# Attention with expert routing: the turned rows of blocks 3 and 4 placed in another step, and a routing written with other instructions

## The chip, the cores and the metric

The kernel runs on one core of one Trainium2 chip. Five engines work side by side and meet through semaphores: TensorE (PE, whose weight loads are listed as PEld), VectorE (DVE), ScalarE (ACT), GpSimd (POOL) and SyncE (SP, which issues most DMAs). The metric is the device time of one execution in microseconds (us).

## What is computed

Attention with rotary positions for 4 batches, 8 heads, 576 tokens and 64 numbers a head, and behind it a sparse feed-forward layer with 8 experts. The reference, cut:

```python
# attention, for every batch and head
q_rot, k_rot = rotate(q), rotate(k)
attn = softmax(q_rot @ k_rot.T / sqrt(64))
x = (attn @ v)            # heads side by side: (4, 576, 512)

# one expert a token
logits = x @ w_gate                      # (4, 576, 8)
local_gate = sigmoid(x @ w_local)        # (4, 576)
for b, s:
    fresh_e = argmax(logits[b, s])
    e = fresh_e if s == 0 or local_gate[b, s] < 0.5 else prev_e
    prev_e = e
    p = softmax(logits[b, s])[e]
    out[b, s] = p * (relu(x[b, s] @ w1[e]) @ w2[e])
```

A token whose local gate is 0.5 or more keeps the expert of the token before it, so the experts of a batch follow from a scan over its 576 tokens.

## The kernel before

**Attention.** Two heads are a pair; there are 16 pairs (4 a batch), and each takes 9 steps, so step g = 0 to 143 is step i = g mod 9 of pair p = g div 9. (Counted from one, i = 5 is the sixth step.) A step makes the scores of one tile of 128 queries by 576 keys (`mm_s`, tile `s`, two PSUM buffers of pool `ps_s`), takes each row's minimum on DVE (`softmax_min`, `mn`; the scores carry a minus sign), the exponential and its row sum on ACT (`softmax_exp`, `e` or `et`, `sum`), turns the exponentials of two steps earlier on PE (`tr_main`, `tm`, `tk`, `tt`), splits them into a high part on ACT (`pth`, `pkh`) and a low part on DVE (`ptl`, `pkl`), and multiplies with the values of the pair before (`pv_mm`, five products a step by `PV_STEPS`, none in i = 8; `pv_evac` adds the halves: `tmp` on ACT, `xt` on DVE). The tiles tm, tk, tt, pv and gx share the four PSUM buffers of pool `ps_t`. POOL rotates and splits the queries, keys and values of coming pairs (`stage`, `xq`, `xk`, `v`).

**Turned rows.** Two pairs later, `gates(p)` divides by the row sums and turns the finished rows back to token order, which also gives the gate logits: `sums` (ACT and a RECIPROCAL on DVE), `rows(0, 3)` for blocks 0 to 2 of 128 tokens and `rows(3, 2)` for blocks 3 and 4. `rows` makes products on PE into a PSUM tile `gx`; for pairs 0 to 10 the first call copies gx on ACT and multiplies on POOL, the second multiplies on DVE from PSUM (`gm`, 36 numbers a partition, then `xrow`, 256). The rows go to DRAM (`rows_d`). The main loop appends these functions to a list `soon` at step `GATES_AT` and takes one from it in each step: before, sums in i = 7, rows(0, 3) in i = 8, rows(3, 2) in i = 0 of the next pair.

**Routing.** When 12 of 16 pairs are turned, `route(0, 3)` routes batches 0 to 2 (15 blocks of 128 tokens) in the steps that the string `ORDER` gives, from g = 121 (pair 13) on and in the drain behind the last step: `fresh` (best expert and the key of each token that doesn't keep its neighbour's), `last_reset` (the scan), `experts` (expert numbers, one-hot, counts), `ranks` (place of each token in its expert's list), `sums`, `probs`, then from `early` the plan of 6 tiles of 128 tokens with one expert each and from `slots` the token numbers of each slot (`gidx` to gather, `sidx` to scatter). `route(3, 1)` does the last batch's 5 blocks during the first experts.

**Experts.** 19 tiles: gather the rows (POOL), turn (`tx`, split to `xs`), first product (`h`), relu, turn (`th`, split to `hs`), second product (`o`), scale, scatter. Weights are loaded by SP and split into two parts by ACT, DVE and POOL (`split_w`).

**Order.** PE's instructions are meant to stand as written; DVE, ACT, POOL and SP are placed by a scheduler between step 12 and the end of attention, and it takes PE's instructions of neighbouring steps out of the written order in some places. PE and DVE stand as written during experts 0 to 5, all engines behind that. Each engine works through its own queue in order, so an instruction that waits holds what is queued behind it.

Of the kernel before, what the change touches and what calls it, by code (L numbers as in the profile page):

```python
# [17 lines left out]
ALU = mybir.AluOpType  # L18
# [6 lines left out]
P = 128  # L25
# [28 lines left out]

ORDER = ".....fs.rRe.klx.c0pt...wg.1.G"
BIG = 4096.0
# [6 lines left out]
ZTHR = -1.5 * 2.0 ** -23  # L63

_COLS = {}
_off = 0
for _n, _w in (
    ("iota128", 128), ("code8", 8), ("p1", 1),
    ("keys", NBLK * NE), ("s0", NBLK), ("pad", NBLK), ("tok64", NBLK),
    ("scan0", 8 * NG + 8), ("tile128", 25),  # L70
):
    _COLS[_n] = (_off, _off + _w)
    _off += _w
# [3 lines left out]
def _constants():  # L77
    c = np.zeros((P, NCONST), np.float32)
    p = np.arange(P)

    def put(name, a):
        lo, hi = _COLS[name]
        if a.dtype == np.int32:
            c.view(np.int32)[:, lo:hi] = a
        else:
            c[:, lo:hi] = a

    put("iota128", np.arange(128)[None])
    put("code8", 7 - np.arange(8)[None])
    put("p1", p[:, None] + 1)  # L90
    tok = np.zeros((P, NBLK))
    tok64 = np.zeros((P, NBLK))
    s0 = np.zeros((P, NBLK))
    pad = np.zeros((P, NBLK))
    s0[0, ::NB] = 1
    pad[:64, 4::NB] = 64
    for b in range(B):
        for j in range(NB):
            lo = b * S + (j * 128 if j < 4 else S - 128)
            tok[:, b * NB + j] = lo + p  # L100
            tok64[:, b * NB + j] = lo // 64
    put("keys", (TWO23 + 8 * tok[:, :, None] + 7 - np.arange(8)).reshape(P, -1))
    put("s0", s0)
    put("pad", pad.astype(np.int32))
    put("tok64", tok64)
# [32 lines left out]
def tile_attention_moe(ctx, tc, qk, v, tabs, turn, consts, tri, wg, wts, out):  # L138
# [17 lines left out]
    cst = const.tile([P, NCONST], F32, name="cst")  # L156
    C = {n: cst[:, a:b] for n, (a, b) in _COLS.items()}
    trib = const.tile([P, P], BF16, name="trib")
# [258 lines left out]
    def gates(p):  # L417
# [48 lines left out]

        def last_rows():
            rows(3, 2)
            for f in stores:
                f()  # L470

        return [sums, lambda: rows(0, 3), last_rows]

    def scores(b):

        g = gm_t[b]
        if b < B - 1:
            pool.tensor_tensor(g[:, :, 0:4], g[:, :, 0:4], g[:, :, 4:8], op=ALU.add)
            pool.tensor_tensor(g[:, :, 0:2], g[:, :, 0:2], g[:, :, 2:4], op=ALU.add)
            pool.tensor_tensor(lg_all[:, b * NB:(b + 1) * NB], g[:, :, 0], g[:, :, 1], op=ALU.add)  # L480
        else:
            dve.tensor_reduce(lg_all[:, 0:NB], g.rearrange("p j h e -> p j e h"), axis=AX.X, op=ALU.add)

    def route(b0, nb):
# [9 lines left out]
        def fresh():  # L494
# [16 lines left out]
            dve.scalar_tensor_tensor(c8, d, 0.0, keys, op0=ALU.is_equal, op1=ALU.mult)  # L511
            rs = blk("rs")
            dve.scalar_tensor_tensor(rs, lg[:, :, 8], ZTHR, C["s0"][:, cs], op0=ALU.is_lt, op1=ALU.max)
            yield
# [3 lines left out]
            key = blk("key")  # L518
            dve.tensor_tensor(key, rs, f, op=ALU.mult)
            yield  # L520
# [23 lines left out]
        def experts():  # L544
# [11 lines left out]

            dve.tensor_scalar(tcode[:, cs], e, -7.0, 4096.0, op0=ALU.add, op1=ALU.mult)
            cnt = small([P, NE, NG + 1], "cnt", BF16)
            dve.tensor_tensor(cnt[:, :, 1:n + 1].rearrange("p e j -> p j e"), bc(C["code8"], 1, n), bc(e, 2, 8), op=ALU.is_equal)
            dve.tensor_tensor(oh, bc(C["code8"], 1, n), bc(e, 2, 8), op=ALU.is_equal)  # L560

# [12 lines left out]
            cox_t[b0] = cox  # L574
            st["cnt"] = cnt

        def sums():
            se = blk("se")
            dve.tensor_reduce(se, st["ex"], axis=AX.X, op=ALU.add)
            yield  # L580
            dve.tensor_scalar(se, se, 1e-9, None, op0=ALU.add)
            yield
            dve.reciprocal(se, se)
            yield
            st["se"] = se

        def probs():
# [3 lines left out]
            p = blk("p")  # L591
            dve.tensor_reduce(p, pm, axis=AX.X, op=ALU.add)
            yield
            dve.tensor_tensor(p, p, st["se"], op=ALU.mult)
# [8 lines left out]
        def ranks():  # L603
# [14 lines left out]
            yield  # L618
            dve.tensor_tensor(o, r, hi, op=ALU.subtract)
            if final:  # L620
# [4 lines left out]
            yield  # L625
            dve.scalar_tensor_tensor(tcode[:, cs], hi, -TWO23, tcode[:, cs], op0=ALU.add, op1=ALU.add)
            yield
# [21 lines left out]
    def slots(codes, nblk, first, n):  # L649
# [3 lines left out]
        def spread_tokens():  # L653
# [9 lines left out]

            dve.tensor_tensor(rhs[:, 0], w, bc(C["tok64"][:, 0:nblk], 2, n), op=ALU.mult)
            dve.tensor_scalar(rhs[:, 1], w, C["p1"], None, op0=ALU.mult)
            yield
            st["rhs"] = rhs

        def gather_tokens():
# [6 lines left out]
            dve.tensor_scalar(hi, ps[:, 0], 64.0, None, op0=ALU.mult)  # L676
            yield
            dve.tensor_tensor(hi, hi, ps[:, 1], op=ALU.add)
            yield
            dve.tensor_copy(gidx[:, first:first + n], hi)  # L680
            pad = small([P, n], "ipad")
# [4 lines left out]

        return [spread_tokens, gather_tokens]

# [25 lines left out]
    take = const.tile([P, NE + 1], F32, name="take")  # L714
    after = const.tile([P, NE], F32, name="after")
    ex_row = const.tile([1, KE + NLATE + 1], F32, name="ex_row")


    def early():
# [4 lines left out]
        def plan():  # L724
# [469 lines left out]
    if True:  # L1194
# [40 lines left out]
        for g in range(NSTEP):  # L1235
            if g == GM:
                begin.close()
            with tc.manual_schedule(engines=None if g < GM else MAN0):
# [152 lines left out]
```

## Time and profile before

| what | value |
| --- | --- |
| median of 3 runs | 541.94 us (541.6 to 542.74) |
| the profiled execution | 541.58 us, span 539.7 us |
| busy PE, DVE, ACT, POOL | 517.0, 381.9, 347.2, 341.3 us (96, 71, 64, 63% of the span) |
| granted TensorE clock | 0.994 of full speed over the span |
| attention, routing 0 to 2, drain | about 0 to 297 us |
| experts, with the routing of batch 3 in the first ones | about 297 to 537 us |

The 541.58 us are the time of the profiled execution, of which the profile's records span 539.7. A busy share of PE near 100% hides little pauses, since the ends of matmuls are modelled; the distance between equal places of two pairs is the surer measure, and a bracket at a row's end gives the idle time ahead of an instruction and what ended it.

### The profile page before, as it was taken

The numbers are of one execution on the slowest core, as the hardware profiler recorded it, in microseconds if no ns is written. First come the engines' busy times: TensorE is split into PE (matmuls) and PEld (weight loads), VectorE is DVE, ScalarE is ACT, GpSimd is POOL, SyncE is SP. The second block draws the span as 40 slices with busy tenths as digits, with TensorE's granted clock in tenths as the row PEclk, the third lists the DMA queues.
The fourth block names the chain that finished last, engine by engine and source line by source line (L and its number), as shares of the span: only waits on it lengthen the run. The fifth ranks groups of instructions, "written<-read, shape, count | busy, mean of one in ns | idle before, by whom it ended". The sixth has DMA issues, their size and how long they took to land.

```text
span 539.7 us, 10708 instructions
## 1 busy us (share of the span) xinstructions
PE 517.0 (96%) x3273; PEld 458.5 (85%) x3273; DVE 381.9 (71%) x703; ACT 347.2 (64%) x762; POOL 341.3 (63%) x267
## 2 busy tenths in 40 slices
PE   7989999999999999998899999999999999999993
PEld 4889999999999999997888788887888888888882
DVE  6998999999999999999999935428422637421631
ACT  4988999999999999987676523353533443532440
POOL 4998989989969989896598302337511455411332
PEclk9999999999999999999999999999999999999997
DMA  8659698887886969977278205471637496637350
GB/s 275 279 132 230 183 246 231 209 192 216 217 229 134 233 189 235 223 189 171 39 200 230 83 20 177 125 267 49 225 103 238 125 353 151 203 100 234 84 172 26
DMA packets 63611, 97.37 MB, mean 180 GB/s; under 512 B 28146, under 2 KB 38898, under 8 KB 61747
## 3 DMA queue, kind: packets, MB, share of 16 engines
q1 hardware_dynamic: 60066, 86.48, 58.1%
q0 software_dynamic: 3040, 9.71, 5.6%
q8 instruction: 28, 0.46, 0.4%
q14 instruction: 45, 0.36, 0.2%
q10 hardware_dynamic: 432, 0.36, 0.2%
HBM read 76.98 MB, written 12.86 MB: 166 GB/s over the span
## 4 chain that ended last, share of the span: by engine, by line
PE 72%; DVE 10%; POOL 5%; DMA 4%; issue 4%; ACT 3%; SPq 1%; POOLq 0%; DVEq 0%; ACTq 0%
PE h L952 18%; PE o L995 17%; PE pv L361 12%; PE s L267 10%; PE tm L325 8%; DVE mn L272 3%; PE gx L435 2%; DVE ptl L307 2%; PE th L986 2%; DMA rows_d<-xrow 2%; PE tx L938 1%; POOL stage L196 1%; PE tk L335 1%; ACT e L289 1%; DMA qst<-xq 1%
## 5 line engine op out<-in xcount | busy, mean ns | idle before, releaser
L995 PE MATMUL o<-w,hs 128*128 128x512 f32 x456 | 112.9, 397 | 0.0
L272 DVE TENSOR_REDUCE mn<-s 128x1 f32<-128x576 f32 x144 | 107.2, 744 | 2.4 <-PE s L267 0.9
L952 PE MATMUL h<-w,xs 128*128 128x512 f32 x444 | 106.1, 392 | 0.8 <-DVE xs L307 0.5
L289 ACT ACTIVATE e<-s,mn 128x576 f32<-128x576 f32 x128 | 95.4, 746 | 14.8 <-DVE mn L272 12.0
L307 DVE TENSOR_TENSOR ptl<-tm,pth 128x512 fp32r<-128x512 f32 x139 | 95.3, 686 | 12.4 <-ACT pth L303 7.4
L1001 POOL DMA_INDIRECT out_dram<-os,sidx x19 | 23.1, 1214 | 123.6 <-ACTq L903 70.3
L267 PE MATMUL s<-m,qst 128*128 128x288 f32 x512 | 95.7, 309 | 4.5 <-ACT e L289 3.0
L952 PEld LDWEIGHTS h<-w,xs 128*128 128x128 f32 x444 | 82.5, 188 | 19.1 <-DVE w L897 1.1
L995 PEld LDWEIGHTS o<-w,hs 128*128 128x128 f32 x456 | 83.0, 188 | 16.9 <-DVE hs L307 0.4
L303 ACT CAST pth<-tm 128x512 fp32r<-128x512 f32 x139 | 80.9, 582 | 12.8 <-PE tm L325 11.8
L267 PEld LDWEIGHTS s<-m,qst 128*128 128x128 f32 x512 | 74.5, 188 | 8.4 <-ACT e L289 5.3
L361 PE MATMUL pv<-pth,v 128*128 128x288 f32 x256 | 76.8, 315 | 2.4 <-DVE pkl L307 1.3
L325 PE MATMUL tm<-wid,e 128*128 128x128 f32 x512 | 77.0, 272 | 0.6 <-ACT e L289 0.5
L361 PE MATMUL pv<-ptl,v 128*128 128x288 f32 x256 | 76.5, 314 | 0.0
L196 POOL TENSOR_TENSOR stage<-stage 128x1152 f32<-128x1152 f32 x26 | 69.1, 2667 | 4.4 <-DMA stage<-in_qk_dram 4.4
L325 PEld LDWEIGHTS tm<-wid,e 128*128 128x128 f32 x512 | 62.1, 140 | 1.2 <-ACT e L289 0.7
L897 DVE TENSOR_TENSOR w<-stage,w 128x1024 fp32r<-128x1024 f32 x37 | 51.0, 1412 | 15.6 <-ACT w L894 9.8
L361 PEld LDWEIGHTS pv<-pth,v 128*128 128x128 f32 x256 | 48.2, 188 | 6.0 <-issue 3.0
L361 PEld LDWEIGHTS pv<-ptl,v 128*128 128x128 f32 x256 | 48.3, 189 | 0.0
L307 DVE TENSOR_TENSOR xs<-tx,xs 128x512 fp32r<-128x512 f32 x19 | 13.1, 688 | 44.6 <-ACTq L903 35.0
L307 DVE TENSOR_TENSOR hs<-th,hs 128x512 fp32r<-128x512 f32 x26 | 17.5, 687 | 30.6 <-ACTq L903 18.9
L197 POOL TENSOR_TENSOR stage<-stage 128x576 f32<-128x576 f32 x26 | 37.0, 1430 | 0.3
(201 smaller groups left out, 821.4 us busy)
## 6 DMA issues: line engine op xcount, KB each, us to landing
stage<-in_wts_dram SPq DMA_DIRECT2D x84, 512.0 KB
stage<-in_qk_dram SPq DMA_DIRECT2D x13, 1152.0 KB
qst<-xq SPq DMA_DIRECT2D x56, 128.0 KB
stage<-in_v_dram SPq DMA_DIRECT2D x16, 320.0 KB
m<-xq SPq DMA_DIRECT2D x14, 288.0 KB
m<-xk SPq DMA_DIRECT2D x14, 288.0 KB
m<-xq SPq DMA_DIRECT2D x14, 256.0 KB
m<-xk SPq DMA_DIRECT2D x14, 256.0 KB
```

The source lines that it names most:

```text
L196: engine.tensor_tensor(x, x, tab[:, 2 * f:2 * f + 2], op=ALU.mult)
L197: engine.tensor_tensor(rr[:, f], x[:, 0], x[:, 1], op=ALU.add)
L267: pe.matmul(st[:, h, lo:hi], lhs, keys[:, k0:k0 + hi - lo], start=(n == 0), stop=(n == len(parts_) - 1))
L272: dve.tensor_reduce(mn, s_t[g][:, :, 0:HALF], axis=AX.XY, op=ALU.min)
L289: act.activation(dst.rearrange("p (h s) -> p h s", h=2), s_t.pop(g)[:, :, 0:HALF], AF.Exp, bias=mn, scale=-1.0, accum_out=sums[:, col:col ...
L303: act.copy(hi, src)
L307: dve.tensor_tensor(lo, src, hi.bitcast(F32), op=ALU.subtract)
L325: pe.transpose(ps[:, k], src[:, k * P:(k + 1) * P], ident)
L361: pe.matmul(pv_t[p, u], lhs.rearrange("p c d -> p (c d)"), rhs, start=(n == 0), stop=(n == 9))
L897: (pool if k in on_pool else dve).tensor_tensor(lo, src, hi.bitcast(F32), op=ALU.subtract)
L952: pe.matmul(ps[:, c], xs_t[t][:, x, k], w[y][:, c * 512:(c + 1) * 512], start=(k == 0 and n == 0), stop=(k == 3 and n == 2))
L995: pe.matmul(ps, hs_t[t][:, x, k], w[y][:, (k % 2) * 512:(k % 2 + 1) * 512], start=(k == 0 and n == 0), stop=(k == 7 and n == 2))
```

## The change

Five things are changed.

1. **The step of the turned rows.** For pairs below `POOL_ROWS` the list is now sums, rows(3, 2), nothing, nothing, rows(0, 3), store; and it is appended at i = 4 instead of 7 (pairs 13, 14 and 15 of the main loop keep their steps). So rows(3, 2) of pair p stands in i = 5 of pair p + 2, rows(0, 3) in i = 8 as before, and the store of its rows in i = 0.
2. **Left out or joined on DVE.** `rs` (a mask with the first token of a batch forced) is gone: the first token's local logit is overwritten by a one-element memset behind `lg_all`, on POOL for batches 0 to 2, and `key` compares and multiplies at once. The early `tcode` is gone: one operation at the end of `ranks` makes the code, with constants moved into `SHIFT` and `lead`. The two products that make `rhs` (tile `ex`, later `slr`) are one, over a constant of two halves.
3. **Moved to ACT.** The one-hot `oha` is a copy of `cnt`, and the 1e-9 is added to `se` there.
4. **Moved to POOL.** `lc` (for batches 0 to 2) and a new one-element `lead`.
5. **Order and types.** `gidx` comes from an addition that writes integers directly, not from a cast of `ihi`; the two operations of `sidx` are a function of their own (`i`, last in ORDER); `iota128` is bf16.

```diff
-ORDER = ".....fs.rRe.klx.c0pt...wg.1.G"
+ORDER = ".....fs.rRe.klx.c0pt...wg.1.Gi"
...
+SHIFT = TWO23 + 7 * 4096.0
...
-        return [sums, lambda: rows(0, 3), last_rows]
+        if p < POOL_ROWS:
+            rest = lambda: None
+            return [sums, lambda: rows(3, 2), rest, rest, lambda: rows(0, 3), lambda: stores[0]()]
+        return [sums, lambda: rows(0, 3), lambda: rows(3, 2)]
...
+            pool.memset(lg_all[0:1, b * NB:b * NB + 1, 8:9], -1.0)
...
-            rs = blk("rs")
-            dve.scalar_tensor_tensor(rs, lg[:, :, 8], ZTHR, C["s0"][:, cs], op0=ALU.is_lt, op1=ALU.max)
...
-            dve.tensor_tensor(key, rs, f, op=ALU.mult)
+            dve.scalar_tensor_tensor(key, lg[:, :, 8], ZTHR, f, op0=ALU.is_lt, op1=ALU.mult)
...
-            dve.tensor_scalar(tcode[:, cs], e, -7.0, 4096.0, op0=ALU.add, op1=ALU.mult)
             cnt = small([P, NE, NG + 1], "cnt", BF16)
             dve.tensor_tensor(cnt[:, :, 1:n + 1].rearrange("p e j -> p j e"), bc(C["code8"], 1, n), bc(e, 2, 8), op=ALU.is_equal)
-            dve.tensor_tensor(oh, bc(C["code8"], 1, n), bc(e, 2, 8), op=ALU.is_equal)
+            act.copy(oh, cnt[:, :, 1:n + 1].rearrange("p e j -> p j e"))
...
-            dve.tensor_scalar(se, se, 1e-9, None, op0=ALU.add)
-            yield
-            dve.reciprocal(se, se)
+            act.add(se, se, 1e-9)
...
             dve.tensor_reduce(p, pm, axis=AX.X, op=ALU.add)
+            dve.reciprocal(st["se"], st["se"])
...
-            dve.tensor_tensor(o, r, hi, op=ALU.subtract)
+            (dve if final else pool).tensor_tensor(o, r, hi, op=ALU.subtract)
...
-            dve.scalar_tensor_tensor(tcode[:, cs], hi, -TWO23, tcode[:, cs], op0=ALU.add, op1=ALU.add)
+            dve.scalar_tensor_tensor(tcode[:, cs], st["e"], 4096.0, hi, op0=ALU.mult, op1=ALU.add)
...
-            dve.tensor_tensor(rhs[:, 0], w, bc(C["tok64"][:, 0:nblk], 2, n), op=ALU.mult)
-            dve.tensor_scalar(rhs[:, 1], w, C["p1"], None, op0=ALU.mult)
+            tokp = C["tokp"].rearrange("p (c j) -> p c j", c=2)[:, :, 0:nblk]
+            dve.tensor_tensor(rhs, bc(w, 1, 2), bc(tokp, 3, n), op=ALU.mult)
...
+            dve.tensor_tensor(gidx[:, first:first + n], hi, ps[:, 1], op=ALU.add)
             dve.tensor_tensor(hi, hi, ps[:, 1], op=ALU.add)
             yield
-            dve.tensor_copy(gidx[:, first:first + n], hi)
+            st["hi"] = hi
+
+        def scatter_tokens():
+            hi = st["hi"]
             pad = small([P, n], "ipad")
...
+            pool.tensor_scalar(lead, take[:, 0:1], SHIFT, None, op0=ALU.add)
...
-                if i == GATES_AT.get(p, 7) and p >= 2:
+                if i == GATES_AT.get(p, 4) and p >= 2:
```

How the instructions stand is shown at three places. The first is PE in steps 2 and 3 of pair 8 (tiles s_75 and s_76), before; pairs 9 to 13 read alike:

```order
L267 MATMUL s_75_2531<-m_8_2179,qst0_99 128x288 x4
L325 MATMUL tm_72_2541<-wid_93,et_8_2453 128x128 x4
L341 MATMUL tt_72_2548<-wid_93,et_8_2453 128x128
L267 MATMUL s_76_2565<-m_8_2179,qst0_99 128x288 x4
L361 MATMUL pv_7_0_2554<-pth_7_2246,v2_7_2009 128x288
L361 MATMUL pv_7_0_2554<-ptl_7_2247,v2_7_2009 128x288
```

The same place now:

```order
L266 MATMUL s_75_2533<-m_8_2189,qst0_99 128x288 x4
L324 MATMUL tm_72_2543<-wid_93,et_8_2463 128x128 x4
L340 MATMUL tt_72_2550<-wid_93,et_8_2463 128x128
L360 MATMUL pv_7_0_2556<-pth_7_2248,v2_7_2011 128x288
L360 MATMUL pv_7_0_2556<-ptl_7_2249,v2_7_2011 128x288
```

The scores s_76 stand behind the five products pv_7_0 again, as they do in pairs 5 to 7 of both kernels.

The second is DVE in steps 0 to 2 of pair 8, before, with the rows of blocks 3 and 4 of pair 5 (gx_5_3); pairs 9 to 13 read alike, and in pair 5 xrow stands right behind gm:

```order
L448 TENSOR_TENSOR gm_1_2120<-gx_5_3_2486,sum_1_1285 128x2x18
L272 TENSOR_REDUCE mn_74_2529<-s_74_2500 128x1
L307 TENSOR_TENSOR ptl_7_2247<-tm_71_2507,pth_7_2246 128x4x128
L307 TENSOR_TENSOR pkl_7_2249<-tk_71_2514,pkh_7_2248 128x256
L272 TENSOR_REDUCE mn_75_2563<-s_75_2531 128x1
L449 TENSOR_TENSOR xrow_5_3_2489<-gx_5_3_2486,sum_1_1285 128x256
```

The same rows of pair 5 now, in step 5 of pair 7:

```order
L371 TENSOR_TENSOR xt_6_2295<-pv_6_1_2321,tmp_6_2296 64x288
L447 TENSOR_TENSOR gm_1_2039<-gx_5_3_2360,sum_1_1294 128x2x18
L448 TENSOR_TENSOR xrow_5_3_2363<-gx_5_3_2360,sum_1_1294 128x256
L271 TENSOR_REDUCE mn_70_2400<-s_70_2373 128x1
L306 TENSOR_TENSOR ptl_7_2249<-tm_67_2379,pth_7_2248 128x4x128
```

Both readers of gx_5_3 stand together, behind xt and ahead of the next minimum; that holds in all 11 pairs.

The third is DVE where the routing of batches 0 to 2 begins, before:

```order
L500 TENSOR_REDUCE mx_3_4212<-lg_all_112 128x15
L513 SCALAR_TENSOR_TENSOR rs_7_4220<-lg_all_112,cst_90 128x15
L272 TENSOR_REDUCE mn_127_4229<-s_127_4192 128x1
L307 TENSOR_TENSOR ptl_13_3982<-tm_124_4199,pth_13_3981 128x4x128
L503 TENSOR_TENSOR d_4_4214<-lg_all_112,mx_3_4212 128x120
L429 RECIPROCAL sum_3_3602<-sum_3_3602 128x10
L511 SCALAR_TENSOR_TENSOR c8_6_4218<-d_4_4214,cst_90 128x120
L516 TENSOR_REDUCE f_8_4222<-c8_6_4218 128x15
L272 TENSOR_REDUCE mn_128_4278<-s_128_4231 128x1
```

The same place now:

```order
L499 TENSOR_REDUCE mx_3_4216<-lg_all_112 128x15
L428 RECIPROCAL sum_3_3613<-sum_3_3613 128x10
L502 TENSOR_TENSOR d_4_4218<-lg_all_112,mx_3_4216 128x120
L510 SCALAR_TENSOR_TENSOR c8_6_4222<-d_4_4218,cst_90 128x120
L271 TENSOR_REDUCE mn_127_4231<-s_127_4196 128x1
L513 TENSOR_REDUCE f_7_4224<-c8_6_4222 128x15
L575 TENSOR_REDUCE se_9_4273<-ex_5_4220 128x15
L306 TENSOR_TENSOR ptl_13_3985<-tm_124_4203,pth_13_3984 128x4x128
L516 SCALAR_TENSOR_TENSOR key_8_4226<-lg_all_112,f_7_4224 128x15
L271 TENSOR_REDUCE mn_128_4279<-s_128_4233 128x1
```

`rs` is gone, and d and c8 have come ahead of the minimum mn_127. On ACT, `ex` (from d) has come ahead of the cast `pth` of tm_124, and the exponential `et` ahead of both.

## Rows read from the trace of the kernel before

**Rows 1.** Stretches: from:to, us; busy time (and instructions) of PE, PEld, DVE, ACT, POOL; clock, DMA, GB/s.

```profile
90.00:105.00 15.00, 15.00 (x119) 14.77 (x118) 14.17 (x27) 13.90 (x35) 14.83 (x11) 1.00 0.78 199
...
255.00:270.00 15.00, 13.59 (x104) 12.27 (x104) 14.47 (x34) 10.05 (x25) 7.73 (x10) 1.00 0.29 56
```

**Rows 2.** Timeline of PE: start us, us, instruction; the tail scores, once a pair.

```profile
75.02 0.96 PE L267 MATMUL s<-xq,qtail 128*128 128x288 f32 x6
91.84 0.96 PE L267 MATMUL s<-xk,qtail 128*128 128x288 f32 x6
...
141.02 0.95 PE L267 MATMUL s<-xq,qtail 128*128 128x288 f32 x6
...
225.14 0.96 PE L267 MATMUL s<-xk,qtail 128*128 128x288 f32 x6
```

**Rows 3.** Timeline of PE, pair 9, steps 2 and 3.

```profile
165.01 0.78 PE L267 MATMUL s<-m,qst 128*128 128x288 f32 x4
165.92 0.37 PE L361 MATMUL pv<-pth,v 128*128 128x288 f32 x1
```

**Rows 4.** Timeline of DVE, pair 9, steps 0 to 2.

```profile
162.75 0.18 DVE L448 TENSOR_TENSOR gm<-gx,sum 128x36 f32<-128x36 f32 x1
...
165.35 0.42 DVE L449 TENSOR_TENSOR xrow<-gx,sum 128x256 f32<-128x256 f32 x1
```

**Rows 5.** Timeline of DVE, pair 4, step 1.

```profile
80.34 0.42 DVE L449 TENSOR_TENSOR xrow<-gx,sum 128x256 f32<-128x256 f32 x1 [0.57 <-DMA rows_d<-xrow]
```

**Rows 6.** DVE by form, 60 to 240 us: count, busy us, mean ns, idle before.

```profile
L449 DVE TENSOR_TENSOR xrow<-gx,sum 128x256 f32<-128x256 f32 x11 | 4.6, 417 | 0.6 <-DMA rows_d<-xrow 0.6
```

**Rows 7.** Timeline of DVE, routing of batches 0 to 2: operations that go or change.

```profile
246.21 1.27 DVE L513 SCALAR_TENSOR_TENSOR rs<-lg_all,cst 128x15 f32<-128x15 f32 x1
...
250.69 0.47 DVE L581 TENSOR_SCALAR se<-se 128x15 f32<-128x15 f32 x1
...
260.05 1.15 DVE L557 TENSOR_SCALAR tcode<-e 128x15 f32<-128x15 int32 x1
...
261.41 0.48 DVE L560 TENSOR_TENSOR oha<-cst,e 128x120 f32<-128x120 f32 x1
...
267.35 0.99 DVE L619 TENSOR_TENSOR lc<-rk,lb 128x15 f32<-128x15 f32 x1
...
279.40 0.99 DVE L664 TENSOR_TENSOR ex<-c,cst 128x90 bf16<-128x90 bf16 x1
...
282.10 0.85 DVE L665 TENSOR_SCALAR ex<-c,cst 128x90 bf16<-128x90 bf16 x1
...
288.34 0.53 DVE L680 CAST gidx<-ihi 128x6 uint32<-128x6 f32 x1
```

**Rows 8.** Timeline of POOL, same stretch.

```profile
246.04 1.41 POOL L207 TENSOR_TENSOR xq<-stage,xq 128x576 fp32r<-128x576 f32 x1
...
259.89 1.28 POOL L300 TENSOR_TENSOR ptl<-stage,pth 128x512 fp32r<-128x512 f32 x1
...
267.03 1.28 POOL L300 TENSOR_TENSOR ptl<-stage,pth 128x512 fp32r<-128x512 f32 x1
```

**Rows 9.** DVE by form, 330 to 335 us: the product of two parts for batch 3.

```profile
L664 DVE TENSOR_TENSOR slr<-slw,cst 128x380 bf16<-128x380 bf16 x1 | 0.6, 554 | 0.0
```

**Rows 10.** Timeline of PE, its longest waits during the routing of batches 0 to 2.

```profile
247.37 0.80 PE L267 MATMUL s<-m,qst 128*128 128x288 f32 x4 [0.74 <-ACT et L289]
...
251.88 0.37 PE L361 MATMUL pv<-pth,v 128*128 128x288 f32 x1 [1.31 <-DVE pkl L307]
...
264.06 1.03 PE L267 MATMUL s<-xk,qtail 128*128 128x288 f32 x6 [0.82 <-issue]
...
281.04 0.44 PE L335 MATMUL tk<-wid,e 128*128 128x128 f32 x2 [0.73 <-DVE ptl L307]
```

**Rows 11.** Timeline of ACT, where that routing begins.

```profile
245.99 0.59 ACT L303 CAST pth<-tm 128x512 fp32r<-128x512 f32 x1 [0.61 <-PE tm L325]
246.48 0.75 ACT L289 ACTIVATE et<-s,mn 128x576 f32<-128x576 f32 x1
```

More of the change, by code (lines that the diff above doesn't have):

```diff
@@ L67 @@
 for _n, _w in (
-    ("iota128", 128), ("code8", 8), ("p1", 1),
-    ("keys", NBLK * NE), ("s0", NBLK), ("pad", NBLK), ("tok64", NBLK),
+    ("iota128", 64), ("code8", 8),
+    ("keys", NBLK * NE), ("pad", NBLK), ("tokp", 2 * NBLK),
     ("scan0", 8 * NG + 8), ("tile128", 25),
@@ L84, in put @@
             c.view(np.int32)[:, lo:hi] = a
+        elif name == "iota128":
+            c.view(np.uint16)[:, 2 * lo:2 * hi] = a.astype(np.float32).view(np.uint32) >> 16
         else:
@@ L89, in _constants @@
     put("code8", 7 - np.arange(8)[None])
-    put("p1", p[:, None] + 1)
     tok = np.zeros((P, NBLK))
     tok64 = np.zeros((P, NBLK))
-    s0 = np.zeros((P, NBLK))
     pad = np.zeros((P, NBLK))
-    s0[0, ::NB] = 1
     pad[:64, 4::NB] = 64
@@ L102, in _constants @@
     put("keys", (TWO23 + 8 * tok[:, :, None] + 7 - np.arange(8)).reshape(P, -1))
-    put("s0", s0)
     put("pad", pad.astype(np.int32))
-    put("tok64", tok64)
+    put("tokp", np.concatenate([tok64, np.broadcast_to(p[:, None] + 1, (P, NBLK))], axis=1))
     sc = np.ones((8, NG + 1))
@@ L156, in tile_attention_moe @@
     cst = const.tile([P, NCONST], F32, name="cst")
-    C = {n: cst[:, a:b] for n, (a, b) in _COLS.items()}
+    C = {n: cst[:, a:b].bitcast(BF16) if n == "iota128" else cst[:, a:b] for n, (a, b) in _COLS.items()}
     trib = const.tile([P, P], BF16, name="trib")
@@ L465, in gates @@
         stores = []
[L467 to L470, printed above, removed]
-        return [sums, lambda: rows(0, 3), last_rows]
+        if p < POOL_ROWS:
+            rest = lambda: None
+            return [sums, lambda: rows(3, 2), rest, rest, lambda: rows(0, 3), lambda: stores[0]()]
+        return [sums, lambda: rows(0, 3), lambda: rows(3, 2)]
     def scores(b):
@@ L480, in scores @@
             pool.tensor_tensor(lg_all[:, b * NB:(b + 1) * NB], g[:, :, 0], g[:, :, 1], op=ALU.add)
+            pool.memset(lg_all[0:1, b * NB:b * NB + 1, 8:9], -1.0)
         else:
             dve.tensor_reduce(lg_all[:, 0:NB], g.rearrange("p j h e -> p j e h"), axis=AX.X, op=ALU.add)
+            dve.memset(lg_all[0:1, 0:1, 8:9], -1.0)
     def route(b0, nb):
@@ L574, in experts @@
             cox_t[b0] = cox
-            st["cnt"] = cnt
+            st.update(cnt=cnt, e=e)
         def sums():
@@ L685, in gather_tokens @@
             yield
-        return [spread_tokens, gather_tokens]
+        return [spread_tokens, gather_tokens, scatter_tokens]
     def tile_experts(inc, first, n):
@@ L715, in tile_attention_moe @@
     after = const.tile([P, NE], F32, name="after")
+    lead = const.tile([P, 1], F32, name="lead")
     ex_row = const.tile([1, KE + NLATE + 1], F32, name="ex_row")
@@ L753, in codes @@
         def codes():
-            st["codes"] = yield from tile_codes(st["t"], st["wgt"], KE, 0.0)
+            st["codes"] = yield from tile_codes(st["t"], st["wgt"], KE, SHIFT)
         def gathers():
@@ L768, in load_more @@
             yield
-        spread_tokens, gather_tokens = slots(lambda: st["codes"], nblk, 0, KE)
-        return {"l": plan, "x": experts_of, "c": codes, "t": spread_tokens, "g": gather_tokens, "G": gathers,
+        spread_tokens, gather_tokens, scatter_tokens = slots(lambda: st["codes"], nblk, 0, KE)
+        return {"l": plan, "x": experts_of, "c": codes, "t": spread_tokens, "g": gather_tokens, "G": gathers, "i": scatter_tokens,
                 "0": lambda: split_first(0), "1": lambda: split_first(1), "w": load_more}
@@ L792, in codes @@
             st["t"] = yield from tile_experts(st["inc"], KE, NLATE)
-            st["codes"] = yield from tile_codes(st["t"], st["wgt"], NLATE, take[:, 0:1])
+            st["codes"] = yield from tile_codes(st["t"], st["wgt"], NLATE, lead)
         def experts_of():
@@ L814, in first_gather @@
             yield
-        return [plan, codes] + slots(lambda: st["codes"], NBLK, KE, NLATE) + [first_gather, experts_of]
+        spread_tokens, gather_tokens, scatter_tokens = slots(lambda: st["codes"], NBLK, KE, NLATE)
+        return [plan, codes, spread_tokens, gather_tokens, first_gather, experts_of, scatter_tokens]
     NTILE = KE + NLATE
```

## The prediction, made before the changed kernel ran

> **What bounds the kernel now.** I read the stretches first [rows 1]. In attention (90 to 105 us) PE is busy for all of 15.00 us, with DVE at 14.17, ACT at 13.90 and POOL at 14.83 behind it: no engine has room, and PE sets the pace. While batches 0 to 2 are routed (255 to 270 us) PE has 13.59, DVE 14.47, ACT and POOL clearly less: here DVE paces. The clock is 1.00 in both, so no time is to be had from it. Next comes the distance between tail scores, which occur once a pair [rows 2]. From 91.84 to 141.02 us lie three pairs (5 to 7) of 16.39 us; from 141.02 to 225.14 five pairs (8 to 12) of 16.82; pair 4 (75.02 to 91.84) also takes 16.82. The work of these pairs is alike, so .43 us are lost in each of the longer ones.
>
> Where, PE's and DVE's timelines of pair 9 tell. DVE makes gm at 162.75, but the second reader of the same gx, xrow, only from 165.35 to 165.77, behind three other instructions [rows 4]. So a quarter of pool ps_t stays held for some 3 us. On PE the scores start at 165.01, end at 165.79, and the first pv product starts only at 165.92, .15 after xrow's end [rows 3]: the products needed that buffer, and the scheduler, which foresaw it, put the scores ahead of them. In pairs 5 to 7, where gm and xrow stand together, the scores stand behind the products and the .43 are absent. In pair 4 xrow waits .57 us for a store of older rows [rows 5]; same loss by another wait.
>
> **Part 1, the turned rows.** Nothing is added: PE makes the same gx, DVE the same 11 gm of .18 us [rows 4] and 11 xrow of .417 [rows 6]. They move from steps 0 to 2 into step 5, adjacent, behind xt. A gx buffer is then held for .18 + .42 and not for 3 us, and PE's order in pairs 8 to 13 becomes that of pairs 5 to 7. Taken away: pair 4, pairs 8 to 12 and pair 13 (same order on both engines), 7 x .43 = **3.0 us**. Bounds: nothing at all (rival B), and 3.3 if pair 3 too loses its like. What is late next is step 5 itself: DVE gets .18 + .42 = .60 us between xt and the next minimum. The minimum feeds ACT's exponential, whose turning is two steps away on PE; that distance is the cover. If it is gone, the .60 fall on PE (rival C). The DMAs move too: the store of rows 3 and 4 is issued by SP in step 5, that of the other three blocks in step 0, still ahead of the loads of values; no reader of rows_d comes before the experts, so I cost this at nothing. What could hurt is an xr buffer not yet stored, as in pair 4; three steps between the two stores, where there was one, make that less likely.
>
> **Part 2, the routing.** What goes from DVE, from its timeline [rows 7]: the addition to `se` .47, `oha` .48, the second product `ex` .85, and `gidx`, a cast of .53, whose work an addition now does; the small gm takes .18 [rows 4], so .35 as an estimate, between nothing and .53. Three more go or change engine: `rs` 1.27, early `tcode` 1.15, `lc` .99. All are of 15 numbers a partition, and gm with 36 takes .18. Each overlaps a POOL instruction and ends with it: xq from 246.04 to 247.45, rs from 246.21 to 247.48; ptl 259.89 to 261.17, tcode 260.05 to 261.20; ptl 267.03 to 268.31, lc 267.35 to 268.34 [rows 8]. So these three don't work for 3.41 us, they wait for POOL's instruction to end. What stands in each place afterwards? d (two SBUF inputs) behind the reciprocal; `cnt`; the new `tcode`. If these begin during the same POOL instruction, they wait in its stead and the 3.41 come back.
>
> The Trainium skill, page "SBUF — State Buffer", section "Who interferes with whom", says this of a VectorE instruction with two SBUF inputs: it shares a port pair with GpSimd, and whichever began first shuts the other out for its whole length. The trace agrees: rs ends .03 us behind xq. By that rule the blocking moves to the next such instruction, and only the work itself is saved; without it all 3.41 would be.
>
> The joined product costs something: 380 elements took .554 us [rows 9], and the bf16 product of 180 about .554 x 180/380 = .26 (estimate), ahead of .99 for the first alone, itself under a POOL instruction [rows 7]. Between -.26 and 0; I take -.26. Sum without the blocked three: .47 + .48 + .85 + .35 - .26 = 1.89 us of DVE; with them 5.3. The end is set by PE, which can give back only what it waits: .74, 1.31, .82 and .73 [rows 10], together 3.6, in four places that end on ACT `et`, DVE `pkl`, its own sequencer and DVE `ptl`. So the routing gives between 1.9 and 3.6; I take **2.3**, near the low end, since the block has a successor in each of the three places.
>
> Edits at nothing. ACT takes `oha` and `se`: between 250 and 270 us it is busy 10.05 of 15 [rows 1], and if that cover failed each would cost up to .5. On ACT `ex` now stands ahead of pth (245.99), and `et` (246.48) ahead of both [rows 11]: the first PE wait (.74, for et) should go, but pth of tm_124 comes some 1 to 2 us later if d is held by POOL, and ptl, then pv behind it. This is the counter-effect that the 2.3 leave room for. POOL takes `lc`, `lead` and a one-element memset; no row shows a POOL operation so small, so between nothing and the 1.28 of a ptl of 512 numbers [rows 8], and I take .3, near nothing for their size. POOL is busy 7.73 of 15 in this part [rows 1], but its one-hots follow `lc`, so it can lengthen the chain to the gathers by .3, which the earlier `gidx` (its successor `sidx` now comes behind) pays back. bf16 in iota128 leaves POOL as it is or makes it faster. The expert phase has PE as its bound; the few DVE operations fewer of batch 3 lie beside it: 0, with ±.3.
>
> **Sum.** 541.58 (profiled execution) - 3.0 - 2.3 = 536.3. The median of the runs lies .36 above the profiled execution, so **536.6**.
>
> **The rivals.** *A: the block moves on whole, or ACT is held.* d, cnt and tcode wait just as long, `ex` on ACT waits for d, pth and ptl are late, and the 1.9 that DVE saves are lost again to a pth that is 1 to 2 us late. For it: the POOL instructions stay; against: 1.9 us of plain DVE work are gone where DVE paces. Routing gives 0: 541.94 - 3.0 = 538.9. By the rule of the Trainium skill named above, this is the natural outcome for the blocked 3.41, not for the 1.9.
>
> *B: the pairs don't shorten.* PE's .43 turn into another wait, e.g. for the exponential that the later minimum in step 5 delays, and only the routing counts: 541.94 - 2.3 = 539.6. For it: ACT is busy 13.90 of 15; against: pairs 5 to 7 do run at 16.39 with the same work.
>
> *C: slower.* Step 5 has no room, and gm and xrow are exposed on PE: .60 x 11 pairs = 6.6 us, against 5.3 gained: 541.94 - 5.3 + 6.6 = 543.2. It decides from 5.3/11 = .48 us a pair. For it: DVE at 14.17 of 15; against: .83 us in 15 are left, and the same .60 were there before, in other steps of the same pair.
>
> *D: the routing gives all.* All four PE waits close, 3.6: 541.94 - 3.0 - 3.6 = 535.3, or 534.8 with .5 from batch 3 and pair 3.
>
> **How the numbers follow.** Forecast .58 (own range 535.4 to 538.0), A .17, B .10, C .06, D .09. Both terms stand on rows with a clear mechanism, so faster has most of it. The range reaches down over D (534.8) and up over A and B (540.0): it leaves out C, and a little at each end for terms that miss together, about .15. A measurement of this kernel tells about 0.2%, 1.1 us, from no change: faster means under 540.9. Faster .90 (all but C and some of B), same .04, slower .06.
>
> **What would show it.** Tail scores 16.4 apart in pairs 4 and 8 to 13, and pv in step 2 without a wait, show part 1 right; a tail distance of 16.8, or a wait on PE in steps 5 to 7 that ends on ACT `e` or DVE `mn`, shows it wrong. In routing, d, cnt and tcode of over .9 us beside a POOL instruction show that the block moved on; about .2 show it gone. PE waits of 3.6 us falling to 1 to 2 show the second term; the distance from the last tail score to the first expert product gives it whole. A pv that waits longer than 1.31 for ptl or pkl would show A. The prediction is wrong if the pairs keep their 16.8, or if the routing stretch is no shorter although DVE has 2 us less to do.

## The result, and the profile of the changed kernel

| what | before | changed |
| --- | --- | --- |
| median (6 runs each) | 542.18 us (541.6 to 542.98) | 546.6 us (545.2 to 546.79) |
| ratio | 1 | 1.007, interval 1.0058 to 1.0083 |
| profiled execution, its span | 541.58, 539.7 us | 546.72, 544.6 us |

The changed kernel is slower by 0.7% (the medians lie 4.4 us apart), where 5.3 us of gain were forecast. Its time lies outside the range of 534.8 to 540.0, on the other side of the kernel before.

By the tail scores of the changed kernel's PE timeline, which answer to [rows 2], and the first product of the experts (`h`), the 4.9 us of the two spans are here:

| stretch, us | before | changed | difference |
| --- | --- | --- | --- |
| span start to tail score of pair 3 | 58.64 | 59.27 | +.63 |
| pairs 3 to 13 | 184.57 | 186.23 | +1.66 |
| pair 14 | 20.85 | 22.27 | +1.42 |
| last tail score to the first `h` | 33.60 | 33.43 | -.17 |
| first `h` to the end of the span | 242.04 | 243.40 | +1.36 |

Three of the tail scores of PE's timeline, which answer to [rows 2]; the first begins pair 5, and from the second to the third is pair 10:

```profile
92.20 0.95 PE L266 MATMUL s<-xk,qtail 128*128 128x288 f32 x6
...
175.95 0.95 PE L266 MATMUL s<-xq,qtail 128*128 128x288 f32 x6
194.12 0.95 PE L266 MATMUL s<-xk,qtail 128*128 128x288 f32 x6
```

Pair by pair (us from one tail score to the next):

| pair | 3 | 4 | 5 | 6 | 7 | 8 | 9 | 10 | 11 | 12 | 13 |
| --- | --- | --- | --- | --- | --- | --- | --- | --- | --- | --- | --- |
| before | 16.38 | 16.82 | 16.40 | 16.40 | 16.38 | 16.81 | 16.85 | 16.82 | 16.82 | 16.82 | 18.07 |
| changed | 16.45 | 16.48 | 16.46 | 17.64 | 16.64 | 16.45 | 16.56 | 18.17 | 17.38 | 16.68 | 17.32 |

Pairs 4, 8 and 9 lose some .3 to .4 us, as forecast. (Pair 2 carries one call of rows(3, 2) more than before, +.47, and pair 13 one less, -.75, so those two are for the most part a shift.) But pairs 6, 10 and 11 gain 1.24, 1.35 and .56, and pair 14, where the routing begins, 1.42. In each of them DVE or PE stands at something that POOL makes. First the three long waits of DVE, from its timeline; none of them is in the kernel before:

```profile
124.14 0.20 DVE L447 TENSOR_TENSOR gm<-gx,sum 128x36 f32<-128x36 f32 x1 [1.43 <-POOL lg_all L477]
...
181.05 0.09 DVE L1245 MEMSET sum<- 128x40 f32 x1 [2.08 <-POOL xrow L448]
...
249.95 0.28 DVE L499 TENSOR_REDUCE mx<-lg_all 128x15 f32<-128x120 f32 x1 [1.56 <-POOL lg_all L477]
250.14 0.20 DVE L428 RECIPROCAL sum<-sum 128x10 f32<-128x10 f32 x1
250.26 0.62 DVE L502 TENSOR_TENSOR d<-lg_all,mx 128x120 f32<-128x120 f32 x1
250.92 1.47 DVE L510 SCALAR_TENSOR_TENSOR c<-d,cst 128x120 f32<-128x120 f32 x1
```

1. Pair 6: the first `gm` of batch 1. Its buffer is that of batch 0, which POOL still sums (`scores`). Before, the first writer was POOL itself (rows(0, 3) came first), so nobody waited; now it is DVE in step 5.
2. Pair 10: the memset of `sum` for batch 3. Its buffer was read last by DVE's xrow; now POOL's xrow reads it last, since rows(0, 3) comes last, and the memset has moved up to just behind a RECIPROCAL. (In the kernel before it stands at 188.10, 13.4 us behind the tail score and not 5.1, and waits for nothing.)
3. Pair 14: `mx` waits for POOL's logits, and then `c` takes 1.47 us beside a POOL instruction (shown with Part 2 below).

What PE makes of these, from its timeline; the bracket is the wait ahead of the row:

```profile
124.81 0.63 PE L324 MATMUL tm<-wid,e 128*128 128x128 f32 x4 [0.57 <-DVE xrow L448]
...
178.68 0.77 PE L266 MATMUL s<-m,qst 128*128 128x288 f32 x4 [0.60 <-ACT xrow L441]
182.69 0.80 PE L266 MATMUL s<-m,qst 128*128 128x288 f32 x4 [0.28 <-ACT e L288]
...
197.02 0.77 PE L266 MATMUL s<-m,qst 128*128 128x288 f32 x4 [0.76 <-ACT xrow L441]
...
253.98 1.08 PE L266 MATMUL s<-m,qst 128*128 128x288 f32 x4 [2.47 <-ACT e L288]
254.86 1.06 PE L324 MATMUL tm<-wid,et 128*128 128x128 f32 x4
```

The last wait is twice as long as the longest of [rows 10], and behind it the same four `tm` products take 1.06 us instead of .60: the windows of that stretch (length, then PE, PEld, DVE, ACT, POOL, clock, DMA, GB/s) show a granted clock of .54, so for most of the time the lower of its two levels (1.2 GHz), after a stretch in which PE was busy 1.53 of 4 us.

```profile
250.00:254.00 4.00, 1.53 (x14) 1.29 (x12) 3.97 (x9) 1.69 (x6) 2.14 (x3) 1.00 0.23 55
254.00:257.20 3.20, 3.20 (x15) 3.19 (x16) 2.85 (x8) 3.07 (x9) 2.61 (x4) 0.54 0.77 178
```

The waits of PE at 178.68 and 197.02 have another origin: there the scores stand at the queries (`qst`) of the next pair. The bracket names ACT's copy of gx, which the scores don't read. Run e12 (below) takes these waits away, and in the trace of e1, the move alone, the one in pair 10 is put down to the DMA of qst:

```profile
179.24 0.78 PE L267 MATMUL s<-m,qst 128*128 128x288 f32 x4 [0.44 <-DMA qst<-xq]
```

POOL's timeline in pair 9, before and then changed:

```profile
155.66 1.15 POOL L206 TENSOR_SCALAR xq<-stage 128x1152 fp32r<-128x1152 f32 x1 [0.24 <-POOL stage L197]
160.62 0.29 POOL L448 TENSOR_TENSOR gm<-xrow,sum 128x54 f32<-128x54 f32 x1 [3.81 <-ACT xrow L442]
160.99 0.84 POOL L449 TENSOR_TENSOR xrow<-xrow,sum 128x384 f32<-128x384 f32 x1
161.78 2.68 POOL L207 TENSOR_TENSOR xq<-stage,xq 128x1152 fp32r<-128x1152 f32 x1
```

```profile
162.21 0.28 POOL L447 TENSOR_TENSOR gm<-xrow,sum 128x54 f32<-128x54 f32 x1 [3.17 <-ACT xrow L441]
162.57 0.84 POOL L448 TENSOR_TENSOR xrow<-xrow,sum 128x384 f32<-128x384 f32 x1
163.38 1.15 POOL L205 TENSOR_SCALAR xq<-stage 128x1152 fp32r<-128x1152 f32 x1
164.61 2.70 POOL L206 TENSOR_TENSOR xq<-stage,xq 128x1152 fp32r<-128x1152 f32 x1
```

Before, the first half of xq stood ahead of gm, and POOL did it while it would have waited for ACT's copy of gx anyway. Now it stands behind, so xq ends 7.9 us after the pair's tail score (159.39), not 6.6 (157.83). SP issues qtail, six m and four qst one after the other behind it, and the last qst is what the scores wait for. The edit says nothing of xq; the scheduler that orders POOL put it there when the rows moved.

### The profile page after: what moved, and what is told of

It reads as the page before. It is cut to its first block, busy times and chain, and to the rows that moved or that the text cites. A ratio compares the mean times of both kernels' runs of the same rounds, so it can differ in the third digit from the quotient of the medians.

```text
span 544.6 us, 10714 instructions
## 1 busy us (share of the span) xinstructions
PE 519.2 (95%) x3273; PEld 459.6 (84%) x3273; DVE 380.1 (70%) x693; ACT 348.4 (64%) x766; POOL 342.1 (63%) x272
```

## The experiments

Every run has its own runs of the kernel before on the same chip; a ratio is to those. "Pairs" is the distance of tail scores; "routing stretch" is from the tail score that begins pair 13 to the first `h` (72.52 us before, 73.02 changed).

**e1, the rows alone; e2, the routing alone.** e1 is the kernel before with these lines, e2 the changed kernel with them undone:

```diff
-        return [sums, lambda: rows(0, 3), last_rows]
+        if p < POOL_ROWS:
+            rest = lambda: None
+            return [sums, lambda: rows(3, 2), rest, rest, lambda: rows(0, 3), lambda: stores[0]()]
+        return [sums, lambda: rows(0, 3), lambda: rows(3, 2)]
...
-                if i == GATES_AT.get(p, 7) and p >= 2:
+                if i == GATES_AT.get(p, 4) and p >= 2:
```

> The kernel before with the move of the turned rows alone (items 2 to 5 of the change left out). Theory P (POOL is behind, and DVE, which works in order, stands three times at an instruction that waits for POOL): the waits of DVE on gm (1.43 us) in pair 6 and on the memset of sum (2.08 us) near the start of pair 10 appear as in the changed kernel, pair 13 starts some 3 us later than before, and the time is 545 to 546 us. Theory S (step 5 has no room for the .60 us of gm and xrow in any of 11 pairs): 548.5 us, with every pair some .6 us longer. Theory R (the routing costs it all, the rows give their 3.0 us): 538.9 us.

> The changed kernel with the turned rows in their old steps (only items 2 to 5 of the change). Theory P: the pairs up to 13 take what they took before, POOL is not behind when the routing starts, and the routing gives 1 to 2 us: 540 to 541 us. Theory R: the routing itself costs; about 546 us or more, with a long wait of PE behind DVE at the start of the routing. Theory S: says nothing of it, 540 to 542 us.

e1: 545.76 us, ratio 1.0064 (1.0048 to 1.0079). The three waits of DVE are there (1.44, 2.03 and 1.50 us), pairs 6 and 10 take 17.67 and 18.12, and PE waits 2.47 us where the routing begins, although the routing is the old one. The move alone makes most of the loss (.64 of .70%; by the medians 3.3 of 4.4 us): theory P. e2: 541.69 us, ratio .9992 (.9974 to 1.0011), no change that can be told. Its routing stretch is 72.24 us, .28 under before, but its profiled execution is a long one (543.87 us, 2.2 above the median). In pair 6 POOL's queue came out in another order there too, and the memset of sum waits .82 us. PE also waits 1.10 us for queries in pair 13, but there POOL's order is that of the kernel before; one DMA of `m` ahead of those queries takes SP 2.66 us (at 218.71), where it took 1.30 before (at 217.46). No run tests that cause.

**e3 and e4, the waits taken away.** Four buffers for `sum`; in e4 also one DVE operation for the logits of batches 0 to 2, in place of POOL's three and its memset:

```diff
-                    sum_t[b] = sm_p.tile([P, H * NB], F32, tag="sum", name=f"sum_{b}")
+                    sum_t[b] = sm_p.tile([P, H * NB], F32, tag="sum", name=f"sum_{b}", bufs=4)
...
-            pool.tensor_tensor(g[:, :, 0:4], g[:, :, 0:4], g[:, :, 4:8], op=ALU.add)
...
+            dve.tensor_reduce(lg_all[:, b * NB:(b + 1) * NB], g.rearrange("p j h e -> p j e h"), axis=AX.X, op=ALU.add)
```

> The changed kernel with four buffers for the tile sum in place of two, so that its memset waits for nobody. Theory P: the wait of 2.08 us on DVE near the start of pair 10 goes, pairs 9 and 10 shorten from 17.42 and 18.33 to some 16.4 to 17.0 us, and the time falls by 1.5 to 2.5 us to 544 to 545 us. Theory S and theory R: no change, 546.6 us.

> As e3, and the logits of batches 0 to 2 summed by one DVE operation in place of three POOL operations (and the one-element memset on DVE), so that DVE no longer waits for lg_all of POOL, neither at gm in pair 6 nor at mx when the routing starts. Theory P: the waits of 1.43 and 1.56 us go too, together with the long wait of PE (2.47 us) that follows the second: 540 to 542 us, about as before or faster. Theory S: 546 us, little gained. Theory R: 546 us or slower, since DVE has 3 operations more.

e3: 545.77 us (1.0055, 1.0035 to 1.0075). The wait on the memset is gone, but only .8 of the 1.5 to 2.5 us came: pair 10 falls from 18.17 to 17.07, and pair 11 stays at 17.51, PE waiting there .90 us for the queries. (The 17.42 and 18.33 of the expectation count pairs from their first step; by tail scores they are pairs 9 and 10 with 16.56 and 18.17.) e4: 541.58 us (.9986, .9974 to .9998): the waits on gm and mx are gone, pair 6 takes 16.53 and the routing stretch 70.64. Some 5 us are back against the changed kernel, as theory P had it.

**e5 to e8, less work for POOL.** Before, the move alone, the routing alone and the whole change, each with the products of the rotation over half of the columns:

```diff
-    def rope_half(engine, f, x):
-        engine.tensor_tensor(x, x, tab[:, 2 * f:2 * f + 2], op=ALU.mult)
+    def rope_half(engine, f, x, n=S):
+        y = x[:, :, 0:n]
+        engine.tensor_tensor(y, y, tab[:, 2 * f:2 * f + 2, 0:n], op=ALU.mult)
...
-            rope_half(pool, f, qkl[:, 2 * f:2 * f + 2])
+            rope_half(pool, f, qkl[:, 2 * f:2 * f + 2], S // 2)
```

> The kernel before with the products of the rotation (line 196 of the kernel before, 2.67 us each, two a pair on POOL) made over half of the columns, so that POOL has some 2.7 us less to do in a pair; half of the rotation is left out. Theory G (a quarter of ps_t held by gx, as the prediction had it, costs .43 us in a pair): pairs 8 to 12 stay at 16.8 us, since POOL was in nobody's way: 541 to 542 us. Theory P (POOL sets the pace of these pairs too): they fall to 16.4, 539 us.

> As e5, with the move of the turned rows alone. If only the lateness of POOL took the gain of the move (theory P with G), the waits on the memset of sum, on gm in pair 6 and on mx go, all pairs from 3 to 12 take 16.4 to 16.5 us, and the time is 2.5 to 3.0 us under e5. If step 5 is too full for gm and xrow (theory S), pairs stay longer than in e5 and the time is above e5.

> As e5, with the new routing alone (items 2 to 5). Theory P: the extra waits that e2 had in pairs 4, 6 and 13 (1.1 us on PE in pair 13) go, and the routing gives the 1.5 to 2.3 us of the prediction: 1.5 to 2.3 us under e5. If the routing gives nothing of itself because POOL's block moves to the next instructions: equal to e5 within .5 us.

> As e5, with the whole change. Theory P with G: both terms show, 4 to 5 us under e5, about 537 us. Theory S or a loss in the change itself: at e5 or above.

The forecasts of whole times are void: other scores choose other experts, and the four kernels take 641.45, 642.8, 642.76 and 644.29 us, some 100 us more behind the first `h`. Only what lies ahead of it is read (us):

| | pairs 4 to 7 | pairs 8 to 12 | pairs 6, 10, 11 | routing stretch | second tail score to first `h` |
| --- | --- | --- | --- | --- | --- |
| e5, before | 65.57 | 84.12 | 16.39, 16.85, 16.82 | 71.21 | 255.89 |
| e6, rows | 66.12 | 83.96 | 16.54, 17.22, 17.01 | 71.01 | 256.67 |
| e7, routing | 65.53 | 84.12 | 16.39, 16.82, 16.84 | 70.88 | 255.45 |
| e8, whole | 65.97 | 84.20 | 16.52, 17.26, 17.32 | 70.47 | 256.11 |

The same stretch is 257.60 before and 260.98 changed with the whole rotation: of the 3.4 us that the change cost there, .2 are left when POOL has room (e8 against e5). So POOL being behind is most of the loss. But the gain doesn't appear either. Pairs 8 to 12 keep 16.82 in e5: the held gx buffer is a cause by itself, as the prediction had it. With the rows moved, pairs 8, 9 and 12 do shorten (16.51, 16.61, 16.61 in e6), while 10 and 11 still stand at the memset (1.09 us) and the queries, and pairs 4 to 7 become .14 us longer each. And the new routing is worth .33 (e7 against e5) to .54 us (e8 against e6), not 2.3.

**e9, e8 with four buffers for sum.**

> e8 (the whole change, half of the rotation left out) with four buffers for the tile sum. Only the attention is read. In e8 pairs 10 and 11 still take 17.26 and 17.32 us and the memset of sum still waits 1.08 us. If that wait is what lengthens them, they fall to 16.5 each and the stretch from the first tail score to the first expert product from 273.7 to 272.1 us. If POOL's late queries do it, they stay above 17 us.

In its one profiled execution the memset waits no more, yet pairs 10 and 11 take 17.22 and 17.39. The second outcome holds: PE stands at the queries.

```profile
177.15 0.78 PE L267 MATMUL s<-m,qst 128*128 128x288 f32 x4 [0.59 <-DMA qst<-xq]
```

POOL has idle time there, in e8 and e9 more than 5 us ahead of gm in pair 9, and still xq comes late, since it is queued behind gm. It is the order, not the amount of work.

**e10, the routing alone with e4's two mendings; e11, the rows moved in pairs 8 to 12 only.**

> The new routing alone (as e2, turned rows in their old steps), with four buffers for sum and the logits of batches 0 to 2 summed on DVE (as e4). Theory P: the waits of e2 on the memset (0.82 us) and of POOL in pair 13 (1.10 us on PE) go, pairs 8 to 12 keep 16.8 us: 540 to 541 us. Were the moved rows of any worth once POOL's waits are gone, e4 (541.6) would be faster than this one by some 1.5 us; were they worth nothing, equal or slower.

> The changed kernel with the rows in step 5 for pairs 8 to 12 alone (older pairs as in the kernel before, where they take 16.39 us), four buffers for sum, and the logits of batch 2 alone summed on DVE. Theory P: pairs 3 to 7 at 16.4, pairs 8 to 12 at 16.5 to 17.4, no wait on gm in pair 6 and none on mx: 540.5 to 541.5 us, faster than e4 by .3 to 1 us.

e10: 541.36 us (.9993, .9982 to 1.0005), a little over the 540 to 541 expected; pairs 8, 9, 11 and 12 at 16.8, the routing stretch 70.83. Equal to e4, so the moved rows are worth nothing in e4 yet. e11: 543.61 us (1.004, 1.0023 to 1.0058), a miss by 2 us: pairs 8 and 9, where the old steps go over into the new, take 18.31 and 19.30 (why, wasn't followed), while pairs 10 and 11 fall to 16.53 and 16.58.

**e12 and e13, xq ahead of gm again.** One POOL copy of one element, which the next instruction overwrites, in the changed kernel (e12) and in e4 (e13):

```diff
+            if engine is pool:
+                pool.tensor_copy(gm_t[b][0:1, j0, 2 * hp, 0:1], xq[0:1, 0, 0, 0:1].bitcast(F32))
             engine.tensor_tensor(gm_t[b][:, j0:j0 + n, heads], pw, bc(rj, 3, 9), op=ALU.mult)
```

> The changed kernel with one added POOL copy of one element from xq to a place of gm that the next instruction overwrites. It ties gm and xrow of the turned rows behind the first part of the split of xq, the order that POOL had in the kernel before in pairs 8 to 13. If POOL's order (gm and xrow ahead of xq) makes the queries late, PE's waits for the DMA of qst (0.6 to 0.9 us at the ends of pairs 9, 10 and 13) go, and 1.5 to 2.5 us of the 4.4 us of loss come back: 544 to 545 us; gm in pair 6 and mx still wait for POOL. If it does not matter, 546.6 us.

> As e12, with four buffers for sum and the logits summed on DVE (as e4). All four waits that the runs have named so far are gone: pairs 8 to 12 at 16.5 to 16.6 us (e4: 16.48, 16.62, 17.86, 16.60, 16.72), about 1.3 us under e4: 540 to 540.5 us, faster than the kernel before. If pair 10 stays over 17 us, its cause is another.

e12: 545.57 us (1.0064, 1.0045 to 1.0084). PE's waits for the queries are gone, pair 11 falls from 17.38 to 16.59, pair 14 from 22.27 to 21.12, and from the second tail score to the first `h` it takes 258.98 instead of 260.98 us. So POOL's order was the cause. The median fell by 1.0 us only, less than the 1.5 to 2.5 expected; the wait where the routing begins is still 2.04 us. e13: 540.86 us (.9984, .9971 to .9996), a little over the 540 to 540.5 expected. Pair 10 is still 17.92, for DVE now stands at its own summing of logits:

```profile
178.19 0.83 DVE L477 TENSOR_REDUCE lg_all<-gm 128x45 f32<-128x360 f32 x1 [0.89 <-POOL gm L449]
```

**e14, the control.** The kernel before with DVE summing the logits:

> The kernel before with the logits of batches 0 to 2 summed by one DVE operation in place of three on POOL, nothing else: the control for e4 and e10. If the stretch from the tail score of pair 13 to the first expert product (72.5 us before, 70.8 in e10, 70.6 in e4) stays at 72 to 72.5 us here, the new routing is worth some 1.7 us where POOL is not in its way. If it falls to 71 us here too, the summing on DVE made it and the new routing is worth under .5 us.

542.13 us (1.0009, .9993 to 1.0024), routing stretch 71.07: the summing on DVE made 1.45 us of the 1.7, and the new routing .24 (71.07 to 70.83). It spares POOL three operations there, so that xq (245.93 to 247.34) ends before `rs` begins, and PE's 1.31 of [rows 10] is gone:

```profile
247.58 0.16 DVE L509 SCALAR_TENSOR_TENSOR rs<-lg_all,cst 128x15 f32<-128x15 f32 x1
```

The same `rs` took 1.27 us in [rows 7] beside xq; its own work is .16. (Pairs 6 and 10 of e14 take 17.05 and 17.52, which eats it.)

**e15, e13 with batch 1 summed by POOL again.**

> As e13, but the logits of batch 1 are summed by POOL again (three operations), so that DVE in pair 10 does not stand at them: in e13 that one DVE operation waited 0.89 us for gm of POOL and pair 10 took 17.92 us. If every wait of DVE on POOL is now named, pair 10 falls to 16.6 to 16.9 us and the time by 1 to 1.3 us under e13: 539.5 to 540 us, faster than the kernel before by .3 to .4%. If pair 10 stays at 17.5 us or more, a cause is not named yet.

540.29 us, ratio .9979 (.9964 to .9994), the lowest median of all and .2% faster than the kernel before; it is .6 us under e13, not the 1 to 1.3 expected. Pair 10 is 16.60, as expected; but now POOL's sum stands between xrow and the second half of xq, and pair 11 takes 17.91:

```profile
194.49 0.77 PE L266 MATMUL s<-m,qst 128*128 128x288 f32 x4 [1.28 <-ACT xrow L441]
```

By the same reading that is the queries again; it wasn't taken away in a run of its own.

## Why the prediction was wrong, step by step

**What bounds the kernel.** The pace of PE and the loss of .43 us in pairs 8 to 12 were read rightly, and e5 keeps it with POOL lightened. (Three readings were slips: four instructions stand between gm and xrow in pair 9, not three; in pair 7 a minimum stands between them too, so that gx is held from 129.23 to 130.57, and the pair still takes 16.38; and the stretch that Part 2 calls 250 to 270 us is that of [rows 1], 255 to 270.) But the first row of [rows 1] has POOL busy 14.83 of 15.00, more than DVE, and the text drew nothing from it. (That stretch is one of POOL's fullest: over pairs 3 to 12 of the kernel before POOL is busy 92% of the time, DVE 93%, ACT 92%, and in pair 9 POOL only 83%.) So POOL is in places a second pacemaker: its results come just in time there, and what makes one of them 1 us late is seen on PE.

**Part 1, forecast -3.0.** The step of the prediction that failed is "what is late next". The prediction looked at DVE's room in step 5 and at SP, and found them cheap. It didn't ask who writes and reads the tiles of the moved step first and last. `gm` got DVE as its first writer, `sum` got POOL as its last reader, and POOL's queue was rearranged though the edit names no line of it; each of the three shows in the orders of the two kernels. Measured, the move costs 3.1 us up to the first `h` (e1: 260.67 us from the second tail score, against 257.60). The mechanism forecast does work: pairs 8 and 9 are shorter by .36 and .29, and in e15 pairs 8 to 10 and 12 by .22 to .33. Pair 4 (-.34) is no proof of it: with the rows in their old steps it takes 16.38 to 16.40 in e5, e7, e10, e11 and e14, so its 16.82 came from the wait for a store of [rows 5], which those kernels don't have. The size was too large even so: .43 were to come back in seven pairs, and pairs 3 and 5 to 7 get .08 to .14 longer where nothing else disturbs them (e15: 16.48, 16.48, 16.54, 16.52; why, no run shows). The bound of 3.3 had nothing under it: pair 3 took 16.38 already.

**Part 2, forecast -2.3.** Measured over the routing stretch: -.24 (e10 against e14), -.28 (e2), -.33 (e7 against e5), -.54 (e8 against e6), and +.07 (the changed kernel against e1, 73.02 against 72.95). By the prediction's own sign, a stretch hardly shorter although DVE has less to do, this part is wrong. One thing went as the text allowed: the 3.41 us of blocked time came back about whole. `cnt` grew from .67 to 1.68, the new `tcode` took the .99 of `lc`, and `c` takes 1.47 where `rs` took 1.27. The rows of `cnt` and `tcode`, DVE and then POOL of the changed kernel (`c` is shown further up), with the xq that `c` stands beside:

```profile
264.27 1.68 DVE L555 TENSOR_TENSOR cnt<-cst,e 128x120 bf16<-128x120 f32 x1
...
271.19 0.99 DVE L621 SCALAR_TENSOR_TENSOR tcode<-e,lb 128x15 f32<-128x15 int32 x1
```

```profile
250.84 1.41 POOL L206 TENSOR_TENSOR xq<-stage,xq 128x576 fp32r<-128x576 f32 x1
...
264.12 1.28 POOL L299 TENSOR_TENSOR ptl<-stage,pth 128x512 fp32r<-128x512 f32 x1
...
270.87 1.29 POOL L299 TENSOR_TENSOR ptl<-stage,pth 128x512 fp32r<-128x512 f32 x1
```

tcode ends .02 us behind POOL's ptl (272.18 and 272.16), `c` .14 behind xq (252.39 and 252.25), `cnt` .55 behind ptl, which is about its own work. The Trainium skill, page "SBUF — State Buffer", section "Who interferes with whom", has it that a VectorE instruction with two SBUF inputs is shut out while a GpSimd one holds the shared port; all three rows agree. So the first half of rival A, the block that moves on whole, is what happened. Its second half, ACT held by `ex`, shows only where `mx` is late: in the changed kernel `ex` waits 2.52 us for `d`, in e10 it waits for nothing, and the routing gives next to nothing in both. The step that failed here is the 1.89 of plain DVE work: it was turned into PE time nearly one for one, though the four waits of [rows 10] are each the end of a chain. From e14 to e10 DVE's busy time in the routing stretch falls by .96 us (67.33 to 66.37), about half of the 1.89, and PE's waits of over .25 us fall from 3.2 to 2.1 us; but the stretch falls by only .24, and from the last tail score to the first `h` every kernel here takes 33.4 to 33.7 us. So most of the work that DVE was spared had lain beside PE's; what took up the rest of PE's shorter waits isn't shown.

**The rivals.** Rival C had the sign and 543.2, but by another mechanism: .60 us of step 5 exposed in each of 11 pairs. Undisturbed pairs show about .1, and the loss sits in four places. Its chance of .06 was far too low for an edit that moves instructions on all five queues of a kernel with four engines over 90% busy.

**The experts, forecast 0 +- .3.** The profiled execution takes 1.36 us more behind the first `h`. The same part takes from 242.0 to 243.1 us in the kernels with the old routing (before, e14, e1) and from 242.3 to 244.2 in those with the new one. What of it belongs to the change isn't settled; one wait on PE (.63 us for ACT's `hs` at 454.95) occurs in the changed kernel's trace and not before.

## What to carry to other kernels

- When a step is moved, list each tile that it touches with its first writer and last reader, and the engine of each, before and now: a wait appears where an in-order engine becomes the first to write what a slower one still reads.
- Read the queue of every engine that is over 90% busy in both orders, for instructions that the edit doesn't name. Here one operation that slid behind two others on POOL cost PE up to .9 us (e3), three kinds of DMA of SP later (qtail, m, qst).
- An operation that takes long because another engine shuts it out is not saved by removing it; look at what stands in its place (here 3.41 us of such time came back).

## What the runs showed of the hardware

- In the changed kernel the granted clock was .54 from 254.0 to 257.2 us, after PE had been busy 1.53 of the 4 us ahead; a wait of 2.47 us so cost more than itself: four `tm` took 1.06 us for .60.
- Small POOL operations took little: a copy of one element .17 us (e13), the one-element memset .09, `lead` .22 and `lc` of 15 numbers .22, where DVE took .99 for `lc` beside ptl. The prediction had put `lc`, `lead` and the memset at .3. What cost PE time in these runs was the order of POOL's queue.
- The bf16 iota128 left POOL as it was: its one-hots of 128 numbers (`ohr`) take .60 us each in both kernels.
